# Overlap rows of v by transfer in row 1, and a later second dilated tile in rows 4 to 7, in a fused attention and MLP kernel

## The chip, the core and the metric

One core of a Trainium2 chip runs the whole program. The metric is the device time of one execution in microseconds; less is better. The figure given for a kernel is the median of several runs. A profile is one further execution, recorded by the hardware profiler; all durations below are from it.

## The reference

Two stages run one after the other. The first is attention with 8 heads of width 64 over 8 sequences of 576 tokens. Heads 0 to 3 look at a sliding window: each token sees itself and the 31 before it. Heads 4 to 7 look at a dilated window: each token sees every fourth token back over 128 tokens, again 32 of them. The second stage is an MLP over all 4608 tokens, from 512 to 2048 and back, with a squared ReLU.

```python
mask_plain = (rel >= 0) & (rel < window)                                   # window = 32
mask_dil = (rel >= 0) & (rel < window * dilation) & (rel % dilation == 0)  # dilation = 4
scores = np.where(masks, scale * q @ k.T, -1e9)
attn = softmax(scores)
x = (attn @ v)            # then (B, H, S, D) -> (B * S, H * D)
h = x @ w_in              # 4608 x 2048
out = (maximum(h, 0) ** 2) @ w_out
```

## The kernel before

**Rows and chunks.** A "row" is one of the 8 sequences of the batch. A "chunk" is 512 of the 4608 tokens, so there are nine. The kernel computes the attention of row b while it runs the MLP of chunk b - 1; the products are in fp16 with fp32 sums.

**How the order is set.** Each engine executes its own instructions in the order in which the program issues them. The MLP of a chunk is a Python generator (`moe_gen`: `mm1_gen`, then `mm2_gen`, `mm2_by_rows_gen` or `mm2_strassen_gen`). `pump(n)` advances it by n steps, and the attention code calls `pump` between its own pieces. A step of mm1 is half of one block of 128 hidden units: two matmuls of 128x512 (L305). Every second step adds the ScalarE activation `rt` (L328) and the VectorE square `g` (L329); two of those steps add sums of g (L338, L339). A step of the second product is four matmuls of 128x256 (L382) from chunk 2 on, which use seven products in place of eight (sums on VectorE: L413, L425, L409; ScalarE copies: L398), and two matmuls of 128x512 (L450) before that. So the number in a `pump` says how much MLP work TensorE, ScalarE and VectorE find between two attention pieces.

**The attention of a row.** `s_sliding` and `s_dilated` compute scores into PSUM tiles `ps` and `pz`; ScalarE takes the exponential into AT (L572), VectorE multiplies by the mask (L575). `av_sliding(b, mp)` multiplies by `vp` into `pav` (L643), two blocks of 96 tokens at a time. `av_dilated(b, t, a)` multiplies by `vd` into `paw` (L659); t is the tile of 80 or 64 positions, a says which two of the four token classes. Both end in `normalize`: a reciprocal (L626) and a product (L631) on VectorE. The PSUM tiles ps, pz, pav and paw, and in row 1 the transposes px and py too, share a pool `pa` of two buffers. Then x is transposed into `xT`, the input of the MLP: rows 0 to 3 on TensorE (L672, L690) with ScalarE copies (L678, L696), rows 4 to 7 by transfer: `x_sliding_by_dma` (L701), and `x_dilated_by_dma` (L708) into tiles `yd`, which `x_from` (L696, ScalarE) puts into xT.

**v and its overlap.** Rows of v arrive from HBM as fp32 in `sv` and `sd` (L132, L137, SP's queue) and GpSimd casts them to fp16 into `vp[b % 2]` (three instructions at L169) and `vd[b % 2]` (four at L177; the first two cover all 128 partitions and write tile 0, the last two 64 partitions of tile 1). A query block also needs keys from the block before it. For sliding heads the last 32 partitions of block m - 1 are repeated in partitions 0 to 31 of block m; for dilated heads the last 64 partitions of tile 0 are repeated in partitions 0 to 63 of tile 1. There are three ways for that in the code:
- `halo_sliding` (L184, three instructions) and `halo_dilated` (L189, two) on ScalarE, called from `attn_scores` and `attn_values`: rows 0, 1 and 2.
- `halo_sliding_by_dma` (L201) and `halo_dilated_by_dma` (L204), one transfer each on SP's queue from on-chip memory to on-chip memory: both in rows 3 and 4, and L204 in rows 5 to 7.
- `halo_sliding_at_end` (L196) on VectorE: rows 5 to 7.

**Around row 1.** GpSimd casts vp, then issues the load of wo (L153) and of row 2's q and k (`ns`, L112), casts vd, and issues the copies of row 2's dilated q and k (`dd`, L214). SP's queue holds row 1's loads of v, and after them the writes of row 2's reordered q and k (L224, behind the VectorE copy L120).

**Rows 4 to 7.** `attn_values_by_dma` issues three sliding pieces with `pump(3)` each, then two dilated tiles t, each with two pieces a:

```python
for t in range(2):
    for a in range(2):
        av_dilated(b, t, a, xs)
        pump(4 + 2 * (a > t))
    ys.append(x_dilated_by_dma(b, t, xs))
    then[1 + t](ys[t])
```

The steps after these four pieces are 4, 6, 4 and 4. `then[1]` loads the next row's sliding v (L132); `then[2]` issues the transposes of its q and k (L232, L236), loads its dilated v (L137) and lets GpSimd cast vp once yd of tile 1 has landed (L914).

Of the kernel before, what the change touches and what calls it, by code (L numbers as in the profile page):

```python
# [17 lines left out]
def kernel(  # L18
# [132 lines left out]
    def load_w_out(gs):  # L151
        for g in gs:
            nc.gpsimd.dma_start(  # L153
                out=wo[g],
                in_=moe_w_out[4 * g * P : 4 * (g + 1) * P, :].rearrange(
                    "(fl s) m -> fl (s m)", s=4
                ),
            )
# [8 lines left out]
    def cast_sliding_v(b, ms=range(0, NB, 2)):  # L167
        for m in ms:
            nc.gpsimd.tensor_copy(  # L169
                vp[b % 2][:, m : m + 2, :, 0:D], sv[:, :, m : m + 2, :].rearrange("p h m d -> p m h d")  # L170
            )

    def cast_dilated_v(b):
        for t in range(2):
            p0 = 64 * t
            for c in range(0, DIL, 2):
                nc.gpsimd.tensor_copy(  # L177
                    vd[b % 2][p0:P, t, c : c + 2, :, 0:D],
                    sd[p0:P, t, :, D * c : D * (c + 2)].rearrange("p h (c d) -> p c h d", d=D),
                )  # L180

    def halo_sliding(b, mp):
        m0, m1 = max(1, 2 * mp), 2 * mp + 2
        nc.scalar.copy(  # L184
            vp[b % 2][0:PADP, m0:m1, :, 0:D], vp[b % 2][P - PADP : P, m0 - 1 : m1 - 1, :, 0:D]
        )

    def halo_dilated(b, c):
        nc.scalar.copy(  # L189
            vd[b % 2][0:64, 1, c : c + 2, :, 0:D], vd[b % 2][64:P, 0, c : c + 2, :, 0:D]  # L190
        )
# [8 lines left out]
    def halo_sliding_by_dma(b):  # L200
        nc.sync.dma_start(out=vp[b % 2][0:PADP, 1:NB], in_=vp[b % 2][P - PADP : P, 0 : NB - 1])  # L201

    def halo_dilated_by_dma(b):
        nc.sync.dma_start(out=vd[b % 2][0:64, 1], in_=vd[b % 2][64:P, 0])  # L204
# [6 lines left out]
    def keep_dilated_qk(b):  # L211
        d = dpool.tile([2, HH * CL, DIL * D], FP16, name=f"dd{b}", tag="dd")
        for i, src in ((1, k), (0, q)):
            nc.gpsimd.dma_start(  # L214
                out=d[i].rearrange("(r i) x -> r (i x)", i=4),
                in_=src[b, HH:H].rearrange("h (r i) d -> (h r) (i d)", i=16),
                max_dma_last_dim=4096,
            )
        return d
# [301 lines left out]
    def pump(n):  # L521
        for _ in range(n):
            while pending:
                try:
                    next(pending[0])
                    break
                except StopIteration:
                    pending.pop(0)
# [52 lines left out]
    def s_sliding(b, hp, between=None):  # L581
        tiles = [pa(f"ps{b}_{hp}_{half}") for half in range(2)]
        for half, ps in enumerate(tiles):
            for m3 in range(3):
                m = 3 * half + m3
                for e in range(2):
                    r = slice(D * e, D * (e + 1))
                    nc.tensor.matmul(  # L588
                        ps[:, e, QB * m3 : QB * (m3 + 1)],
                        QKTp[b % 2][r, 1, hp, QB * m : QB * m + P],  # L590
                        QKTp[b % 2][r, 0, hp, PADP + QB * m : PADP + QB * (m + 1)],
                        start=True,
                        stop=True,
                    )
        for half, ps in enumerate(tiles):
            exps(2 * hp + half, ps)
            if not between:
                masked(2 * hp + half, maskp)
        if between:
            between()  # L600
            for half in range(2):
                masked(2 * hp + half, maskp)

    def s_dilated(b, g):
        tiles = [pa(f"pz{b}_{g}_{h}") for h in range(2)]
        for h, ps in enumerate(tiles):
            for a in range(2):
                for t in range(2):
                    q0 = KPAD + (2 * g + h) * CL + Q0D[t]
                    for e in range(2):  # L610
                        r = slice(D * e, D * (e + 1))
                        o = CL * a + Q0D[t]
                        nc.tensor.matmul(  # L613
                            ps[:, e, o : o + QD[t]],
                            QKTd[b % 2][r, 1, a, q0 - PADD[t] : q0 - PADD[t] + P],
                            QKTd[b % 2][r, 0, a, q0 : q0 + QD[t]],
                            start=True,
                            stop=True,
                        )
        for h, ps in enumerate(tiles):  # L620
            softmax(4 + 2 * g + h, ps, maskd)
# [11 lines left out]
    def x_tiles(b):  # L633
        x = xp.tile([QB, 2, NB, 2, D], FP16, name=f"xs{b}", tag="xs")
        return x, [xp.tile([QD[t], DIL, HH, D], FP16, name=f"xd{b}_{t}", tag=f"xd{t}") for t in range(2)]

    def av_sliding(b, mp, xs):
        pav = pa(f"pav{b}_{mp}")
        for i in range(2):
            m = 2 * mp + i  # L640
            for h in range(HH):
                off = (h % 2) * 288 + (m % 3) * QB
                nc.tensor.matmul(  # L643
                    pav[:, i, h * (D + 2) : h * (D + 2) + D + 1],
                    AT[:, 2 * (h // 2) + m // 3, off : off + P],
                    vp[b % 2][:, m, h, 0 : D + 1],
                    start=True,
                    stop=True,
                )
        normalize(  # L650
            b, f"p{mp}", pav, QB, xs[0][:, :, 2 * mp : 2 * mp + 2].rearrange("p c m e d -> p m c e d")
        )
# [30 lines left out]
    def x_dilated(b, t, xs, wide):  # L683
        py = pt(f"py{b}_{t}", wide)
        w = QD[t]
        for r in range(DIL):
            x = xs[1][t][:, r].rearrange("p h d -> p (h d)")
            for c in range(2):
                o = w * (2 * r + c)
                nc.tensor.transpose(py[:, o : o + w], x[:, P * c : P * (c + 1)], ident[0:w, 0:w])  # L690
        x_from(b, t, py[:, 0 : 8 * w].rearrange("x (r c i) -> x r c i", r=DIL, c=2))
# [21 lines left out]
    def attn_scores(b, gap, less=0, hooks={}):  # L713
        for hp in range(2):
            s_sliding(b, hp)
            if hp in hooks:
                hooks[hp]()
            pump(gap)
        for g in range(2):
            s_dilated(b, g)  # L720
            if 2 + g in hooks:
                hooks[2 + g]()
            if g and b < 3:
                halo_sliding(b, 0)
            pump(gap - less)

    def attn_values(b, gap, wide=False, then=None):
        xs = x_tiles(b)
        for mp in range(3):
            av_sliding(b, mp, xs)  # L730
            if b < 3:
                if mp < 2:
                    halo_sliding(b, mp + 1)
                else:
                    halo_dilated(b, 0)
            if then and b == 2 and mp == 2:
                then()
            pump(gap)
        x_sliding(b, 0, xs, wide)
        if b < 3:  # L740
            halo_dilated(b, 2)
        pump(gap)
        av_dilated(b, 0, 0, xs)
        if then and b == 1:
            then()
        pump(gap)
        x_sliding(b, 1, xs, wide)
        pump(gap)
        av_dilated(b, 0, 1, xs)
        pump(gap)  # L750
        for a in range(2):
            av_dilated(b, 1, a, xs)
            pump(gap)
        x_dilated(b, 0, xs, wide)
        pump(gap)
        x_dilated(b, 1, xs, wide)

    def attn_values_by_dma(b, then):
        xs = x_tiles(b)
        for mp in range(3):  # L760
            av_sliding(b, mp, xs)
            if mp == (2 if b > 4 else 1):
                then[0]()
            pump(3)
        x_sliding_by_dma(b, xs)
        ys = []
        for t in range(2):
            for a in range(2):
                av_dilated(b, t, a, xs)
                pump(4 + 2 * (a > t))  # L770
            ys.append(x_dilated_by_dma(b, t, xs))
            then[1 + t](ys[t])
        pump(6)
        x_from(b, 0, ys[0])
        pump(7)
        x_from(b, 1, ys[1])
# [34 lines left out]
    nc.gpsimd.tensor_copy(sd[64:P, :, :, 0], wi[2][64:P, :, 0:2].rearrange("p d f -> p f d"))  # L811
    load_v(1)
    cast_sliding_v(1)
    load_w_out((3,))
    ns = load_sliding_qk(2)
    cast_dilated_v(1)
    dd = keep_dilated_qk(2)
    for mp in (1, 2):
        av_sliding(0, mp, xs)
# [135 lines left out]
```

## Time and profile before

| | us |
|---|---|
| median of 4 runs (lowest, highest) | 306.76 (305.39, 308.54) |
| the profiled execution's own time | 308.54 |
| its span | 306.8 |
| PE, DVE, ACT, POOL busy | 288.4, 208.7, 173.1, 63.6 |
| halo copies on ScalarE, L184 x9, mean | 0.539 |
| halo copies on ScalarE, L189 x6, mean | 0.616 |

The span is that of the instructions; the time of an execution includes what lies around it. PE is TensorE's matmuls, PEld its weight loads, DVE VectorE, ACT ScalarE, POOL GpSimd, SP the engine that issues most transfers. A row of a timeline gives the start and the length in us, the engine, the line, the operation with output and inputs, how many instructions were merged, and in brackets the idle time before it with what ended that. Lengths of merged rows overlap a little with the next. The row of a window gives from and to, the length, then for each engine the busy time and the number of instructions, the granted TensorE clock, the busy share of the DMA engines and what they moved in GB/s.

Row 1's attention lies at about 49 to 63 us, row 4's at 131 to 153, row 5's at 161 to 189, row 6's at 192 to 219, and row 7's at 222 to 249. From 251 us on only the MLP is left.

### The profile page before, as it was taken

What the parts mean: (1) busy time and instruction counts of PE and PEld (TensorE: products, weight loads), DVE (VectorE), ACT (ScalarE), POOL (GpSimd) and SP (SyncE); (2) the same over time, 40 slices, a digit from 0 to 9 for tenths busy, and PEclk for the clock granted to TensorE, in tenths of its full rate; (3) what the DMA queues carried; (4) which work ended last, traced back from release to release, by engine and by line L of the source; (5) the groups of instructions that cost most, each with busy time, mean ns of one, the idle gap of its engine ahead of it and who ended that gap; (6) DMA issues with size and microseconds to landing.
All of it is one profiled execution on the core that took longest, in us unless ns stands there. A gap on an engine that the chain in (4) does not pass through costs nothing.

```text
span 306.8 us, 6890 instructions
## 1 busy us (share of the span) xinstructions
PE 288.4 (94%) x2760; PEld 192.8 (63%) x2760; DVE 208.7 (68%) x437; ACT 173.1 (56%) x293; POOL 63.6 (21%) x112
## 2 busy tenths in 40 slices
PE   1869999999999999999999999999999999999994
PEld 1444545455555458855888988558855975785583
DVE  7753445858961789579948994899489934834652
ACT  2943656677844883396439534954396347425620
POOL 4435008001431710530026002600230000000000
PEclk9995999999999999999999999999999999999999
DMA  7699997699979999996799999998993230003004
GB/s 121 132 228 215 205 197 124 107 223 224 155 168 192 251 174 206 179 259 128 144 131 282 178 148 189 273 177 167 156 268 20 51 119 28 2 1 137 2 1 137
DMA packets 77471, 46.77 MB, mean 152 GB/s; under 512 B 58432, under 2 KB 69184, under 8 KB 77440
## 3 DMA queue, kind: packets, MB, share of 16 engines
q1 hardware_dynamic: 68688, 32.71, 51.5%
q0 software_dynamic: 8752, 13.63, 25.9%
q8 instruction: 21, 0.34, 0.5%
q14 instruction: 10, 0.08, 0.1%
HBM read 36.70 MB, written 16.52 MB: 173 GB/s over the span
## 4 chain that ended last, share of the span: by engine, by line
PE 65%; DMA 14%; DVE 9%; SPq 4%; ACT 3%; issue 2%; POOL 1%; DVEq 0%; POOLq 0%
PE ph L305 29%; PE pa L382 14%; PE pb L382 7%; PE po L450 6%; DMA sd<-in_v_dram 4%; DMA QKTp<-dp 4%; PE pc L382 3%; DVE g L329 3%; DMA nd<-in_q_dram 2%; DMA ns<-in_q_dram 2%; DMA vd<-vd 2%; PE paw L659 2%; ACT AT L572 1%; PE ps L588 1%; DVE AT L575 1%
## 5 line engine op out<-in xcount | busy, mean ns | idle before, releaser
L305 PE MATMUL ph<-xT,wi 128*128 128x512 f16 (+1 forms) x640 | 136.6, 363 | 0.7 <-ACT xT L696 0.7
L328 ACT ACTIVATE rt<-ph 128x512 f16<-128x512 f32 x144 | 86.3, 609 | 47.1 <-PE ph L305 44.0
L305 PEld LDWEIGHTS <-wi 128*128 128x128 f16 x640 | 68.6, 114 | 47.9 <-issue 3.7
L329 DVE TENSOR_TENSOR g<-rt 128x512 f16<-128x512 f16 x144 | 62.7, 447 | 40.2 <-ACT rt L328 39.0
L382 PEld LDWEIGHTS <-g 128*128 128x128 f16 x448 | 43.3, 98 | 6.2
L382 PEld LDWEIGHTS <-gs 128*128 128x128 f16 x336 | 32.0, 98 | 5.1 <-DVE gs L339 1.6
L450 PE MATMUL po<-wo,g 128*128 128x512 f16 x128 | 33.1, 379 | 0.0
L382 PE MATMUL pa<-wt,gs 128*128 128x256 f16 x224 | 27.6, 273 | 0.8 <-DVE gs L339 0.7
L409 DVE TENSOR_TENSOR ov<-pb,ov 128x512 f32<-128x512 f32 x14 | 9.7, 691 | 25.8 <-ACT ov L398 13.1
L382 PE MATMUL pb<-wt,g 128*128 128x256 f16 x224 | 27.1, 273 | 0.0
L169 POOL CAST vp<-sv 128x512 f16<-128x512 f32 x24 | 15.0, 656 | 53.7 <-DMA sv<-in_v_dram 42.1
L398 ACT COPY ov<-pa 128x512 f32<-128x512 f32 x14 | 8.2, 585 | 31.0 <-PE pa L382 31.0
L177 POOL CAST vd<-sd 128x512 f16<-128x512 f32 (+1 forms) x32 | 21.6, 703 | 14.5 <-DMA sd<-in_v_dram 12.4
L631 DVE TENSOR_TENSOR xd<-paw,rcp_d 80x512 f16<-80x512 f32 (+1 forms) x32 | 21.9, 684 | 1.1
L572 ACT ACTIVATE AT<-pz 128x576 f16<-128x576 f32 x32 | 19.7, 695 | 1.1 <-PE pz L613 1.1
L572 ACT ACTIVATE AT<-ps 128x576 f16<-128x576 f32 x32 | 19.2, 657 | 1.8 <-PE ps L588 1.3
L575 DVE TENSOR_TENSOR AT<-AT,maskp 128x576 f16<-128x576 f16 x32 | 15.1, 480 | 5.4 <-ACT AT L572 3.7
L575 DVE TENSOR_TENSOR AT<-AT,maskd 128x576 f16<-128x576 f16 x32 | 16.7, 543 | 2.5 <-ACT AT L572 0.9
L631 DVE TENSOR_TENSOR xs<-pav,rcp_p 96x512 f16<-96x512 f32 x24 | 16.5, 687 | 0.8
L659 PEld LDWEIGHTS <-AT 128*128 128x128 f16 x256 | 12.1, 98 | 7.3 <-issue 2.4
L398 ACT COPY ou<-pa 128x512 f32<-128x512 f32 x14 | 8.2, 586 | 14.0 <-PE pa L382 14.0
L450 PEld LDWEIGHTS <-g 128*128 128x128 f16 x128 | 10.4, 98 | 8.3
(81 smaller groups left out, 274.6 us busy)
## 6 DMA issues: line engine op xcount, KB each, us to landing
sv<-in_v_dram SPq DMA_DIRECT2D x14, 288.0 KB, 5.5
dp<-nr SPq DMA_DIRECT2D x12, 288.0 KB, 3.9
out_dram<-ou SPq DMA_DIRECT2D x6, 512.0 KB, 4.1
out_dram<-ov SPq DMA_DIRECT2D x6, 512.0 KB, 4.5
sd<-in_v_dram SPq DMA_DIRECT2D x8, 320.0 KB, 6.3
ns<-in_k_dram POOLq DMA_DIRECT2D x8, 288.0 KB, 6.4
ns<-in_q_dram POOLq DMA_DIRECT2D x8, 288.0 KB, 7.5
sd<-in_v_dram SPq DMA_DIRECT2D x8, 256.0 KB, 6.5
```

Source lines behind the costliest of these rows:

```text
L169: nc.gpsimd.tensor_copy(vp[b % 2][:, m : m + 2, :, 0:D], sv[:, :, m : m + 2, :].rearrange("p h m d -> p m h d"))
L177: nc.gpsimd.tensor_copy(vd[b % 2][p0:P, t, c : c + 2, :, 0:D], sd[p0:P, t, :, D * c : D * (c + 2)].rearrange("p h (c d) -> p c h d", d=D),)
L305: nc.tensor.matmul(ph[:, t0:t1], wi4[ffc // 4][:, dmk, :, ffc % 4], xT[:, dmk, x0 : x0 + t1 - t0], start=(dmk == 0 and t0 == 0), stop=(dmk ...
L328: nc.scalar.activation(rt, ph[:], ACTF.Relu)
L329: nc.vector.tensor_mul(g[:, ffc, :], rt, rt)
L382: nc.tensor.matmul(banks[bank][:, t], a(k, t), b(k), start=(new and t == 0 and k == 0), stop=(k == HF - 1), skip_group_check=True,)
L398: nc.scalar.copy(ot, banks[A])
L450: nc.tensor.matmul(po, g[:, ffc, t * P : (t + 1) * P], wo[ffc // 4][:, ffc % 4, :], start=(ffc == 0), stop=(ffc == NFF - 1),)
L572: nc.scalar.activation(AT[:, u, 0:UW], ps[:, :, 0 : UW // 2], ACTF.Exp, scale=scale)
L575: nc.vector.tensor_mul(AT[:, u, 0:UW], AT[:, u, 0:UW], mask)
L631: nc.vector.tensor_tensor(out=x, in0=pv, in1=rb, op=ALU.mult)
L659: nc.tensor.matmul(pav[:, e, h * (D + 2) : h * (D + 2) + D + 1], AT[:, 4 + h, off : off + P], vd[b % 2][:, t, 2 * a + e, h, 0 : D + 1], st ...
```

## The change

It has two parts. In row 1 the five ScalarE copies of the overlap are no longer issued; two transfers on SP's queue, the ones that rows 3 and 4 use, take their place, each issued in the program right after the cast that it reads. In rows 4 to 7 the steps after the four dilated pieces become 7, 3, 4 and 4: the second piece, with its normalization and the transfer that follows it, comes three steps later in the program; the third and the fourth stay at the same step.

```diff
@@ attn_scores
-            if g and b < 3:
+            if g and b == 2:
                 halo_sliding(b, 0)
             pump(gap - less)
@@ attn_values
             av_sliding(b, mp, xs)
-            if b < 3:
+            if b == 2:
                 if mp < 2:
                     halo_sliding(b, mp + 1)
                 else:
...
         x_sliding(b, 0, xs, wide)
-        if b < 3:
+        if b == 2:
             halo_dilated(b, 2)
@@ attn_values_by_dma
                 av_dilated(b, t, a, xs)
-                pump(4 + 2 * (a > t))
+                pump((7, 3)[a] if t == 0 else 4)
@@ the program's order, row 1
     load_v(1)
     cast_sliding_v(1)
+    halo_sliding_by_dma(1)
     load_w_out((3,))
     ns = load_sliding_qk(2)
     cast_dilated_v(1)
+    halo_dilated_by_dma(1)
     dd = keep_dilated_qk(2)
```

## The prediction

> **What bounds the kernel now.** I read the page first, then TensorE's idle time stage by stage, then each engine's timeline through row 1 and rows 4 to 7. The page's first row, and two stages from the table by window:
>
> ```profile
> PE 288.4 (94%) x2760; PEld 192.8 (63%) x2760; DVE 208.7 (68%) x437; ACT 173.1 (56%) x293; POOL 63.6 (21%) x112
> ...
> 49.00:64.50 15.50, 14.59 (x180) 7.44 (x180) 10.51 (x23) 11.41 (x21) 3.88 (x7) 1.00 0.82 163
> ...
> 140.00:155.00 15.00, 15.00 (x145) 11.26 (x142) 13.79 (x29) 7.20 (x11) 0.00 (x0) 1.00 0.66 125
> ```
>
> TensorE is the bound. Its idle time is 306.8 - 288.4 = 18.4 us, of which 14 - 6.62 + 12 - 8.25 = 11.1 us lie before 26 us and 56.2 - 52.1 = 4.1 us in the last window; only 3.2 us is left between. Row 1 (49 to 64.5 us) holds 0.91 us of it. In rows 4 to 7 (130 to 250.6 us) it is 1.0 us: the windows show 0.27, 0.40 and 0.34 us, in stages 155-172, 172-190 and 203-221. Nothing that a change in these two places hides can give more than these sums, plus gaps that the busy row covers.
>
> There are such gaps. The Trainium skill (Trainium Kernel Development and Optimization, section Performance Expectations) says that matmul busy time judges distance to the roofline badly, since matmuls are pipelined. The row bears it out in row 1: from 55.56 to 62.70 us pairs of L450 need 0.43 us by the chain, yet the next group starts 0.06 to 0.23 us later, seven times, 0.94 us together. By the busy row, row 1 could give 0.91 us; by the rule and the starts, 1.85 us. I use the starts, but only as far as the engine behind the gaps, VectorE, can move.
>
> **Row 1: what goes.** Five ScalarE copies, L184 three times and L189 twice: 1.44 + 0.62 + 0.61 = 2.67 us of ScalarE. What stands in their way is seen in the timelines of PE, ACT, DVE and POOL:
>
> ```profile
> 54.18 0.29 PE L643 MATMUL pav<-vp,AT 128*128 128x65 f16 x4
> 55.01 0.29 PE L643 MATMUL pav<-vp,AT 128*128 128x65 f16 x4 [0.54 <-ACT vp L184]
> ...
> 52.25 2.28 ACT L572 ACTIVATE AT<-pz 128x576 f16<-128x576 f32 x4 [0.27 <-PE pz L613]
> 54.55 1.44 ACT L184 COPY vp<-vp 32x256 f16<-32x256 f16 x3
> ...
> 52.93 2.09 DVE L575 TENSOR_TENSOR AT<-AT,maskd 128x576 f16<-128x576 f16 x4 [0.40 <-ACT AT L572]
> 55.33 0.20 DVE L626 RECIPROCAL rcp_p<-pav 96x8 f32<-96x8 f32 x1 [0.31 <-PE pav L643]
> ...
> 45.60 1.72 POOL L169 CAST vp<-sv 128x512 f16<-128x512 f32 x3 [16.61 <-DMA sv<-in_v_dram]
> ...
> 49.02 2.83 POOL L177 CAST vd<-sd 128x512 f16<-128x512 f32 x4
> ```
>
> Block 0 of pav needs no overlap; block 1 waits 0.54 us for the first L184, which stands behind four exponentials. Without it pav ends about 54.18 + 0.43 = 54.6. But VectorE masks until 52.93 + 2.09 = 55.02, so its reciprocal moves from 55.33 to 55.02: **0.31 us**, not 0.54. From there VectorE and its PSUM buffers set the pace to the end of the row: it runs without a break to 57.93, paw starts at 58.08 on the buffer then freed, and the normalizations follow one another to 62.6 (rcp_d 60.05, 60.90, 61.73). So the row ends 0.31 us earlier. ScalarE's later copies wait for TensorE (0.98 and 0.45 us idle before the two L678), so its freed time buys nothing more. L120 (59.38) moves with VectorE; its input needs to have landed by 59.07, and landed at 48.41 + 6.9 = 55.3.
>
> **Row 1: what comes.** Two transfers on SP's queue. SP issues nothing between 41.05 (L137) and 60.15 us (L224), so nothing stands behind their waits: L224 needs L120, not SP. No other queue is passed. vp may go when the three L169 casts end, 47.3; vd when the two 128-row L177 casts end, about 50.4 (row 5 shows this: casts from 166.28 take 1.59 us for two, and L204 goes at 167.90). The same transfers of rows 3 to 7, L201 and then L204:
>
> ```profile
> DMA to landing us min/median/max: 2.9/2.9/3.0
> ...
> DMA to landing us min/median/max: 2.4/4.5/7.6
> ```
>
> The DMA engines moved 0 to 41 GB/s from 47 to 49 us, so vp is near its own row: landing 47.4 + 3.0 = 50.4, needed at 54.4, 4.0 us to spare; even at 7.6 it lands at 55.0, where L184 delivers now. vd goes out amid wo, ns and dd (about 200 GB/s from 50 to 58 us). The rule against taking the long row is the Trainium skill's round-robin (DMA: Bandwidth & Descriptors, section Queues, rings and completion order): each DMA engine changes queues after a packet, so a small transfer passes a backlog on another queue. By that, 132 KB at half of 200 GB/s takes 1.3 us, and on top of the 2.4 us of the emptiest row that is a landing at 54.1. Row 5's L204, with ns and dd of the same size ahead, took 7.6 us: 50.4 + 7.6 = 58.0. I take the row. vd is read by the third paw, at 60.29 now and 59.98 then: 5.9 us to spare by the rule, 2.0 by the row. Both give 0 us, but only the row leaves the cover thin. The reverse side, that 215 KB more delays wo, ns and dd, is 215/400 = 0.5 us at the 400 GB/s of such copies, inside 3.8 us of slack (55.3 to 59.07).
>
> From 62.7 us TensorE is dense, and the chain of row 2 (L184 at 84.58, L120 at 86.43, L224, the transposes, 0.47 us of PE wait at 102.96) hangs on row 1's end and moves with it. **Row 1: -0.31 us**; between -1.85 (all gaps) and +1.7 (vd at the 11.5 us that dd<-in_q needed in row 5: 61.9, 2.0 late, less 0.31).
>
> **Rows 4 to 7: what moves.** Steps 25 to 34 lie between the first and third paw: 25 to 32 are the last four ffc of mm1 (L305, L328, L329), 33 and 34 the start of L382. Now 4 and 6 of them stand around the second paw, then 7 and 3. Eight matmuls, their reciprocal and product (L626, L631), one transpose on SP (L708) with the L132 loads and later L708 behind it: nothing is added. TensorE's order changes, not its sum. On VectorE the normalization passes exactly one L329 (step 30's). Row 5's order:
>
> ```profile
> 177.46 0.75 DVE L329 TENSOR_TENSOR g<-rt 128x512 f16<-128x512 f16 x2
> 178.12 0.20 DVE L626 RECIPROCAL rcp_d<-paw 80x8 f32<-80x8 f32 x1
> 178.35 0.69 DVE L631 TENSOR_TENSOR xd<-paw,rcp_d 80x512 f16<-80x512 f32 x1
> 178.96 0.75 DVE L329 TENSOR_TENSOR g<-rt 128x512 f16<-128x512 f16 x2
> ```
>
> VectorE is 2 to 3 us behind TensorE there: the paw of 175.09 is normalized at 178.12. Moved by 3 x 0.43 = 1.3 us it would be done near 176.8, still ahead of VectorE. The g that now starts at 178.96 has its rt by 177.02. So no bubble opens; the sequence L329, L338, L339, L413 after it ends when it did. The two PE waits on L339 stay:
>
> ```profile
> 181.22 1.48 PE L382 MATMUL pa<-wt,gs 128*128 128x256 f16 x12 [0.40 <-DVE gs L339]
> ...
> 183.98 1.31 ACT L696 COPY xT<-yd 128x640 f16<-128x640 f16 x1 [0.66 <-DMA yd<-xd]
> 186.23 0.58 ACT L398 COPY ov<-pa 128x512 f32<-128x512 f32 x1 [0.94 <-PE pa L382]
> ```
>
> What is late is yd0, by one L329, 0.33 us: L708 at 179.99, L696 ending 185.62 instead of 185.29. The L398 after it waits for TensorE until 186.23, so 0.94 us of cover becomes 0.61. If it were gone, the next product (186.91) would wait for its bank. L132 behind L708 ends by 183.0, before yd1's L708 at 183.98. The fourth paw (179.97) needs the second's buffer, free at 179.3 instead of 178.96. **0 us**; bounds -1.0 (every wait there gone) and +1.2 (yd0 late by the whole 1.3 us, 0.3 us of PE in each of the four rows).
>
> **Sum.** -0.31 + 0 = -0.3 us. The profiled execution took 308.54 us (span 306.8); it becomes 308.2. The runs' median is 306.76, and the same step gives **306.4 us**. A measurement here tells about 1% (3 us) from no change.
>
> **Rivals.** (1) *The forecast*: 305.9 to 306.8, chance 0.57. (2) *Hidden anyway*: vp lands as late as L184 did, or VectorE's backlog eats the 0.31 us: 306.8; the PE gap at 54.5 speaks against it. With noise around it, 0.18. (3) *Better cover*: ScalarE free at 54.5 and L329 earlier also close gaps behind VectorE and the L339 waits, down to 306.76 - 0.91 - 1.0 = 304.9; against it, VectorE's work is the same. 0.13. (4) *vd late, the slower side*: the third paw waits for the transfer. It decides from a landing of 59.98 - 50.4 = 9.6 us. At 11.5 us the time is 308.4; at the 14.3 us of nd<-in_q in the backlog at 25 us, landing at 64.7, 4.7 - 0.3 = 4.4 us worse, 311.2. For it: SBUF copies beside the same loads went from 2.4 to 7.6 us. Against: 14.3 us came with wo, ns and nd queued ahead, 2 x 512 + 3 x 288 KB = 1.9 MB, against some 1.1 MB here (0.56 of wo and ns left, and 0.58 of dd). 0.12.
>
> The range, 304.9 to 308.4, takes in (1) to (3) and the milder (4). Faster by over 1% would need all 3.2 us of mid-kernel idle: 0.03. Slower by over 1% is the worse half of (4) and something unseen: 0.08. Within 1%: 0.89.
>
> **What would show it.** Right: L184 x6, L189 x4, L201 x3, L204 x6; no PE wait for vp in row 1; rcp_p following maskd at once; vd landed before the third paw; row 1 ending 0.3 us earlier; in rows 4 to 7 the second paw 1.3 us later, yd0's L708 0.3 us later, the PE waits on L339 unchanged. Wrong: a PE wait on DMA vd or vp, a new PE idle after 130 us, or rows 2 and 3 not keeping row 1's gain.

## The result, and the profile after

Over 43 runs of the changed kernel and 64 of the one before, the medians are 306.29 and 306.43 us, and the ratio is 0.9996 with a 95% interval from 0.9980 to 1.0012: -0.1 us, give or take 0.5. No difference can be told. The forecast of -0.3 us lies in that interval, but so does nothing at all, and the profile says that for row 1 it was nothing: the wait of TensorE that was to go is still there, with another name. The page's first row, then row 1 on TensorE, VectorE, GpSimd and SP's queue of the changed kernel:

```profile
PE 287.5 (95%) x2760; PEld 192.7 (64%) x2760; DVE 210.2 (69%) x437; ACT 170.6 (56%) x288; POOL 62.1 (20%) x112
```

```profile
46.28 0.43 PE L588 MATMUL ps<-QKTp 64*128 64x96 f16 x12
...
51.34 0.29 PE L643 MATMUL pav<-vp,AT 128*128 128x65 f16 x4
52.22 0.29 PE L643 MATMUL pav<-vp,AT 128*128 128x65 f16 x4 [0.59 <-DMA vp<-vp]
```

```profile
50.10 2.33 DVE L575 TENSOR_TENSOR AT<-AT,maskd 128x576 f16<-128x576 f16 x4
52.55 0.20 DVE L626 RECIPROCAL rcp_p<-pav 96x8 f32<-96x8 f32 x1
```

```profile
44.80 1.72 POOL L169 CAST vp<-sv 128x512 f16<-128x512 f32 x3 [16.14 <-DMA sv<-in_v_dram]
...
48.22 3.16 POOL L177 CAST vd<-sd 128x512 f16<-128x512 f32 x4
```

```profile
46.55 0.60 SPq L201 DMA_DIRECT2D vp<-vp  x1
49.83 0.54 SPq L204 DMA_DIRECT2D vd<-vd  x1
```

The answers on these two lines in row 1, vp first:

```profile
DMA to landing us min/median/max: 5.6/5.6/5.6
```

```profile
DMA to landing us min/median/max: 5.9/5.9/5.9
```

Two things are to be seen. The vp transfer took 5.6 us instead of 3.0, landed at 52.2, and pav's second block waited 0.59 us for it (0.54 for ScalarE before). And VectorE's masks now end at 52.43, 6.15 us after the row's first score matmul; in the first profile of before it was 55.02 - 49.12 = 5.90 us. The reciprocal starts 0.12 us after them, so 0.59 us of wait on TensorE cost VectorE 0.1 us, or 0.2 by comparison with e0 below, where the reciprocal starts 0.08 us ahead of the recorded end of the masks.

In rows 4 to 7 the order on VectorE is the predicted one, with exactly one more L329 ahead of the second normalization (row 5):

```profile
173.65 1.08 DVE L329 TENSOR_TENSOR g<-rt 128x512 f16<-128x512 f16 x3
174.66 0.20 DVE L626 RECIPROCAL rcp_d<-paw 80x8 f32<-80x8 f32 x1
174.89 0.69 DVE L631 TENSOR_TENSOR xd<-paw,rcp_d 80x512 f16<-80x512 f32 x1
175.50 0.41 DVE L329 TENSOR_TENSOR g<-rt 128x512 f16<-128x512 f16 x1
```

and TensorE waits on L339 as it did:

```profile
177.42 1.48 PE L382 MATMUL pa<-wt,gs 128*128 128x256 f16 x12 [0.48 <-DVE gs L339]
...
207.88 1.48 PE L382 MATMUL pa<-wt,gs 128*128 128x256 f16 x12 [0.48 <-DVE gs L339]
```

The profiled spans, 306.8 before and 303.1 after, are not the change. At row 1's first score matmul the two executions were 49.12 - 46.28 = 2.84 us apart already, mostly for a reason that the first experiment shows. So the kernels are compared below by two stretches of TensorE's timeline: "row 1" from the first L588 of row 1 to that of row 2, and "rows 4 to 7" from the first L588 of row 4 to chunk 7's first L305. A third column gives where in row 1 the first reciprocal starts, counted from the row's first L588. Each ratio is taken against runs of before that were made beside it.

| kernel | row 1, us | first reciprocal, us | rows 4 to 7, us | ratio to before (95%) |
|---|---|---|---|---|
| before, first profile | 24.81 | 6.21 | 119.30 |  |
| before, profiled again (e0) | 25.05 | 6.46 | 119.28 |  |
| changed kernel | 24.87 | 6.27 | 119.32 | 0.9996 (0.9980 to 1.0012) |
| e1, transfers of row 1 alone | 26.07 | 7.47 | 120.54 | 1.0006 (0.9966 to 1.0046) |
| e2, steps of rows 4 to 7 alone | 25.12 | 6.53 | 120.00 | 0.9981 (0.9959 to 1.0003) |
| e3, vp transfer in three pieces | 25.05 | 6.47 | 119.69 | 1.0011 (0.9974 to 1.0047) |
| e4, no overlap in row 1 | 25.10 | 6.52 | 119.51 | 0.9984 (0.9960 to 1.0008) |
| e5, steps 10, 0, 4, 4 | 25.21 | 6.57 | 129.20 | 1.0317 (1.0270 to 1.0364) |
| e7, steps 8, 2, 7, 1 and e3 | 25.19 | 6.60 | 119.72 | 1.0009 (0.9986 to 1.0032) |
| e8, casts ahead of the loads | 26.73 | 5.83 | 119.34 | one run |
| e9, e4 with the casts behind the masks | 24.42 | 5.82 | 120.51 | one run |
| e10, half of the casts behind the masks, and e3 | 25.44 | 6.05 | 118.92 | 0.9976 (0.9955 to 0.9997) |

One stretch of one profile moves by some tenths from execution to execution, up to 1.2 us in rows 4 to 7 (e1, e9), in part by a wait of up to 0.7 us on QKTp at a row's start that comes and goes; a difference below that is read here only where a line carries it.

The first two columns belong together. In ten of the twelve profiles the rest of row 1, from its first reciprocal to row 2's first score matmul, takes 18.6 us (18.58 to 18.64). It is longer only in e8 (20.9) and e10 (19.4), where L120 had to wait for its input ns. So row 1 is as long as its first reciprocal is late, as the prediction had it ("from there VectorE and its PSUM buffers set the pace"), and the question is only what that reciprocal waits for.

### The profile page after: what moved, and what is told of

Read it like the earlier page. It is cut to its first block, busy times and chain, and to the rows that moved or that the text cites. A ratio compares the mean times of both kernels' runs of the same rounds, so it can differ in the third digit from the quotient of the medians.

```text
span 303.1 us, 6885 instructions
## 1 busy us (share of the span) xinstructions
PE 287.5 (95%) x2760; PEld 192.7 (64%) x2760; DVE 210.2 (69%) x437; ACT 170.6 (56%) x288; POOL 62.1 (20%) x112
## 4 chain that ended last, share of the span: by engine, by line
PE 64%; DMA 17%; DVE 11%; issue 2%; ACT 2%; SPq 1%; POOL 1%; DVEq 0%; POOLq 0%
PE ph L305 26%; PE pa L382 15%; PE pb L382 8%; DMA sv<-in_v_dram 6%; PE po L450 5%; DMA wi<-in_moe_w_in_dram 5%; PE pc L382 3%; DMA ns<-in_q_dram 3%; DVE g L329 3%; DMA vp<-vp 2%; PE paw L659 2%; DMA QKTp<-dp 2%; DVE AT L575 1%; PE pav L643 1%; DVE gs L338 1%
## 5 line engine op out<-in xcount | busy, mean ns | idle before, releaser
L305 PE MATMUL ph<-xT,wi 128*128 128x512 f16 (+1 forms) x640 | 134.2, 359 | 0.7 <-ACT xT L696 0.7
L305 PEld LDWEIGHTS <-wi 128*128 128x128 f16 x640 | 68.1, 114 | 45.9 <-issue 0.6
L329 DVE TENSOR_TENSOR g<-rt 128x512 f16<-128x512 f16 x144 | 62.6, 447 | 37.5 <-ACT rt L328 36.3
L631 DVE TENSOR_TENSOR xd<-paw,rcp_d 80x512 f16<-80x512 f32 (+1 forms) x32 | 21.9, 684 | 1.1
L575 DVE TENSOR_TENSOR AT<-AT,maskd 128x576 f16<-128x576 f16 x32 | 18.1, 592 | 2.7 <-ACT AT L572 1.6
L631 DVE TENSOR_TENSOR xs<-pav,rcp_p 96x512 f16<-96x512 f32 x24 | 16.5, 687 | 0.8
```

Of the source, the lines that this page charges most:

```text
L305: nc.tensor.matmul(ph[:, t0:t1], wi4[ffc // 4][:, dmk, :, ffc % 4], xT[:, dmk, x0 : x0 + t1 - t0], start=(dmk == 0 and t0 == 0), stop=(dmk ...
L329: nc.vector.tensor_mul(g[:, ffc, :], rt, rt)
L575: nc.vector.tensor_mul(AT[:, u, 0:UW], AT[:, u, 0:UW], mask)
L631: nc.vector.tensor_tensor(out=x, in0=pv, in1=rb, op=ALU.mult)
```

## The experiments

**e0: the kernel before, profiled once more.**

> The kernel before, profiled once more. In its first profile TensorE ran at a granted clock of 0.85 from 26 to 42 us (64 matmuls of chunk 0 in 15.4 us), in the profile of the changed kernel at 1.00 (13.1 us). Theory A (the cover of the transfer was lent by that slow stretch): with a full clock the span is near 304 us, the three vp casts of row 1 end at or after row 1's first score matmul (46.5 against 46.3 in the changed kernel, where the first profile of before had them 1.8 us ahead), and the wait of pav for the ScalarE copy is still 0.5 us, since ScalarE has the casts' result long before. Theory B (the later cast comes from the change): the casts end 1.5 to 2 us ahead of the first score matmul here too.

The stage from 26 to 42 us, of the first profile of before and then of this one:

```profile
26.00:42.00 16.00, 16.00 (x64) 7.54 (x64) 6.38 (x15) 9.53 (x16) 1.50 (x4) 0.85 1.11 213
```

```profile
26.00:42.00 16.00, 16.00 (x143) 8.18 (x142) 7.93 (x18) 10.00 (x18) 0.34 (x2) 1.00 1.11 210
```

Row 1 of e0 on TensorE and on VectorE:

```profile
45.78 0.43 PE L588 MATMUL ps<-QKTp 64*128 64x96 f16 x12
...
51.67 0.29 PE L643 MATMUL pav<-vp,AT 128*128 128x65 f16 x4 [0.54 <-ACT vp L184]
```

```profile
49.60 2.72 DVE L575 TENSOR_TENSOR AT<-AT,maskd 128x576 f16<-128x576 f16 x4
52.24 0.19 DVE L626 RECIPROCAL rcp_p<-pav 96x8 f32<-96x8 f32 x1
```

The third number from the end is the granted clock: 0.85 then, 1.00 here. The 60 matmuls of chunk 0 in this stage, then and here:

```profile
25.98 15.41 PE L305 MATMUL ph<-xT,wi 128*128 128x512 f16 x60 [0.73 <-ACT xT L696]
```

```profile
24.95 13.11 PE L305 MATMUL ph<-xT,wi 128*128 128x512 f16 x60 [0.67 <-ACT xT L696]
```

That is 2.3 us of the 3.34 by which TensorE reaches row 1 earlier here; the other 1.0 us lay ahead of these matmuls. But v arrives only 0.64 us earlier: the vp casts start at 44.96, 0.82 us ahead of the first score matmul, where they were 3.52 us ahead in the first profile. Theory A holds against B in kind (the casts still end after the first score matmul, at 46.68), and it brings the second finding: here the ScalarE copy makes pav wait 0.54 us too, and **VectorE doesn't wait for it at all**. Its masks end at 52.32, later than pav. The 0.31 us that the prediction wanted to save was not there in this execution of the kernel before. What lowered the clock in the first one is not shown.

**e1: the transfers of row 1 alone.** The changed kernel with `pump(4 + 2 * (a > t))` as before.

> Row 1's transfers alone, with the steps of rows 4 to 7 as before. Theory A: the vp transfer goes out together with the loads of wo and ns and lands 5 to 6 us after its issue; pav waits 0.5 to 0.6 us for it as it waited for ScalarE; ratio 0.998 to 1.002. Theory B (the steps of rows 4 to 7 cost what row 1 gains): no wait of pav on the transfer, ratio 0.999 or less, and lower than that of the whole change.

```profile
51.43 0.29 PE L643 MATMUL pav<-vp,AT 128*128 128x65 f16 x4
53.52 0.29 PE L643 MATMUL pav<-vp,AT 128*128 128x65 f16 x4 [1.80 <-DMA vp<-vp]
```

```profile
53.84 0.20 DVE L626 RECIPROCAL rcp_p<-pav 96x8 f32<-96x8 f32 x1 [0.62 <-PE pav L643]
```

The landing took 5.6 us again, as A says, but the wait is 1.8 us and not 0.6, since in this execution v came later still (casts from 46.10, 0.27 us ahead of the first score matmul). Here the wait is longer than what VectorE's masks cover, the reciprocal waits 0.62 us, and row 1 takes 26.07 us, 1.0 more than in e0. The same transfers in e5 (below) make pav wait 0.90 us and VectorE 0.03. So in these three profiles row 1's transfer is between free and a loss of 1 us; what differs is how early v arrives and how late the masks end. B falls: without the new steps there is no gain either.

**e3: the vp transfer in three pieces, each behind its cast; e4: no overlap in row 1 at all.**

```diff
-    cast_sliding_v(1)
-    halo_sliding_by_dma(1)
+    for m in range(0, NB, 2):
+        cast_sliding_v(1, (m,))
+        m0 = max(1, m)
+        nc.sync.dma_start(
+            out=vp[1][0:PADP, m0 : m + 2], in_=vp[1][P - PADP : P, m0 - 1 : m + 1]
+        )
```

> The whole change, with row 1's vp transfer cut in three, each issued right after the cast that it needs: blocks 1, then 2 and 3, then 4 and 5. Theory A: the first piece goes out about 1.1 us earlier, ahead of the loads of wo and ns, lands in about 2.5 us and the wait of pav is gone; the reciprocal follows the last mask at once, row 1 from its first score matmul to the first of row 2 takes 24.87 - 0.3 us = 24.6 us or less; ratio 0.998 to 0.9995. Theory C (the transfer is slow in itself, from 32 partitions to 32): the first piece takes over 5 us too, and pav waits for 0.2 us or more.

> Leaves out the overlap of v in row 1 altogether (zeros are put there long before), so row 1's first keys are missing; all else as in the changed kernel. The upper limit of what row 1's overlap can give: no wait of pav, row 1 to row 2 in 24.5 us against 24.87, ratio 0.998 to 0.9995 by both theories. If it is the same as the changed kernel within 0.05%, then the third of a microsecond is given back to the transfers of row 2 and 3 (a wait on QKTp at row 3's start); if it is faster by 0.3% or more, then the forecast undervalued what stands behind VectorE in row 1.

The landings of e3's three pieces, and its pav:

```profile
DMA to landing us min/median/max: 1.9/2.1/5.0
```

```profile
51.24 0.42 PE L643 MATMUL pav<-vp,AT 128*128 128x65 f16 x8
51.92 0.42 PE L643 MATMUL pav<-vp,AT 128*128 128x65 f16 x8
53.66 0.41 PE L643 MATMUL pav<-vp,AT 128*128 128x65 f16 x8 [0.89 <-issue]
```

The wait of pav is gone, as A says; the first two pieces land in about 2 us, from 32 partitions to 32, so C falls. The third, issued 0.26 us after the load of wo, takes 5.0. But the row takes 25.05 us, no less: the reciprocal comes at 6.47 us, at the end of the masks, as in e0 (6.46), and the third pav now waits 0.89 us; it starts where VectorE's first normalization ends, which frees a PSUM buffer. In e4 there is no overlap to wait for; the reciprocal comes at 6.52, and the row takes 25.10 us. **The 24.5 to 24.6 us that Theory A of e3 and both theories of e4 expected came in neither.** In these executions row 1 has nothing to give to this change: its first reciprocal waits for VectorE's own masks.

**e9: why VectorE is late.** e4, with the dilated casts behind row 1's masks:

```diff
     attn_scores(1, 2, 1)
+    nc.gpsimd.tensor_copy(seen, AT[:, 7, 0:1])
+    cast_dilated_v(1)
```

> Leaves out the overlap of v in row 1 (as one kernel before it), and starts row 1's four dilated casts on GpSimd only after the last mask of the row. Theory A (GpSimd's cast slows VectorE's masks from 0.46 to 0.86 us, and that, not the overlap, sets when row 1's first reciprocal can start): all eight masks take 0.44 to 0.50 us, the reciprocal starts 5.2 to 5.6 us after the row's first score matmul instead of 6.2 to 6.5, if TensorE's pav lets it. Theory B (the masks are slowed by the loads that come in at that time): they stay at 0.7 to 0.86 us with no cast beside them.

The masks of row 1 (minimum, median and maximum in ns), in e0 and then in e9:

```profile
L575 DVE TENSOR_TENSOR AT<-AT,maskp x4: 458/692/857, 46.8 to 48.8; 128x576 f16<-128x576 f16 x4
L575 DVE TENSOR_TENSOR AT<-AT,maskd x4: 447/822/859, 49.6 to 51.9; 128x576 f16<-128x576 f16 x4
```

```profile
L575 DVE TENSOR_TENSOR AT<-AT,maskp x4: 457/458/459, 47.9 to 49.8; 128x576 f16<-128x576 f16 x4
L575 DVE TENSOR_TENSOR AT<-AT,maskd x4: 457/458/459, 50.7 to 52.3; 128x576 f16<-128x576 f16 x4
```

Theory A holds: beside GpSimd's casts a mask takes up to 0.86 us; with the casts out of the way all eight take 0.46, though the loads of wo and ns come in as before and the copies of dd 2 us earlier. The casts are shorter too, 2.41 us for the four instead of 3.01 in e4. The row takes 24.42 us, 0.68 less than e4, and the reciprocal comes 0.70 earlier, at 5.82: a little later than expected, since VectorE now waits 2.0 us for ScalarE's exponentials (1.2 in e4). In e8 (next), where the casts end earlier in the row and the overlap is moved in full, the reciprocal comes at 5.83 as well.

One thing stays open: not every slow mask lies beside a cast in the trace. The second of e0 (0.70 us) and the first of the changed kernel (0.88) lie beside GpSimd's issuing of loads, and beside such issuing the first four masks of e9 took 0.46.

The Trainium skill states the mechanism (SBUF — State Buffer, section Who interferes with whom): a VectorE instruction with two inputs in SBUF contends with a GpSimd instruction that reads SBUF. The masks have two such inputs, the casts read sd. In e9 the casts run from 52.98 to 55.39 beside the normalizations L631, whose first input is in PSUM, and those keep their 0.69 us.

**e8: why the vp transfer was slow.** The order casts, then loads:

```diff
     halo_sliding_by_dma(1)
-    load_w_out((3,))
-    ns = load_sliding_qk(2)
     cast_dilated_v(1)
     halo_dilated_by_dma(1)
+    load_w_out((3,))
+    ns = load_sliding_qk(2)
```

> The changed kernel with row 1's dilated casts and both overlap transfers issued ahead of the loads of wo and ns, which come about 3 us later. It tells why the vp transfer landed 5.6 us after its issue although the DMA engines moved under 60 GB/s then. Theory A (the loads of wo and ns, issued by GpSimd in the same microsecond, hold it up): with none of them under way vp lands in 1.9 to 3.0 us, pav does not wait for it, and vd lands in under 3.5 us. Theory B (it is held up by GpSimd's casts, which run in this order too): vp still takes 4.5 us or more. By both, ns comes late, VectorE's L120 may wait for it by about 1 us, and the time says little.

vp, then vd:

```profile
DMA to landing us min/median/max: 2.1/2.1/2.1
```

```profile
DMA to landing us min/median/max: 3.3/3.3/3.3
```

Theory A: 2.1 and 3.3 us in place of 5.6 and 5.9, with the casts running as before. The loads of wo and ns hold the transfer up, although the DMA engines moved no more than 22, 33 and 49 GB/s in the three microseconds from 46 to 49 in the changed kernel. The trace shows when it lands: with wo. In the six profiles in which wo's load was issued within 0.3 us of vp's transfer or of its last piece, the two landed within 0.25 us of each other. Why the engines moved so little at first stays open. ns came late, as expected, and more than expected: L120 waited 2.24 us for it, TensorE 2.30 us, and the row took 26.73 us.

**e2: the steps of rows 4 to 7 alone,** with row 1 as before.

> The steps 7, 3, 4, 4 of rows 4 to 7 alone, row 1 as before. Theory A (the moved piece changes an order, not a sum): from row 4's first score matmul to the first matmul of chunk 7 it takes 119.3 us as in the profile of before and of the changed kernel (119.30 and 119.32); the second paw 1.3 us later, the yd0 transpose 0.3 us later against the third paw; TensorE waits on L339 in rows 5 and 6 by 0.3 to 0.5 us as before; ratio 0.998 to 1.002. Theory B (the later tile frees VectorE where TensorE waits for it): L339 waits below 0.2 us and a ratio of 0.997 or less.

The waits on L339 are 0.39 and 0.48 us, and nothing else of rows 5 and 6 is shorter: B falls. The stretch is 120.0 us, 0.7 above what A expected; 0.34 us of it is a wait on QKTp at row 5's start, which the changed kernel did not have in the same rows. Row 1, as before, repeats e0: pav waits 0.54 us for L184, and VectorE doesn't wait, since its masks end 0.4 us after pav.

**e5: the cover in rows 4 to 7, taken away.** Steps 10, 0, 4, 4.

> The changed kernel with the second dilated piece moved to the end of its room: steps 10, 0, 4, 4. It tells whether the cover that the prediction named in rows 4 to 7 is real, and which part of it ends first. Theory A: the second normalization now also passes the last two L329, L338, L339 and L413 (0.33 x 2 + 0.73 x 2 + 1.14 = 3.3 us later than in before), so it frees its buffer 2.5 to 3 us after the fourth paw wants it: TensorE waits there 2 to 3 us in each of the rows 4 to 7, the waits on L339 are gone, and the time grows by 7 to 12 us (ratio 1.02 to 1.04). Theory B (VectorE's backlog is not what orders this): the fourth paw waits under 0.5 us and the time grows by under 2 us.

```profile
149.16 0.41 PE L659 MATMUL paw<-vd,AT 128*128 128x65 f16 x8 [1.84 <-DVE rcp_d L626]
...
181.68 0.41 PE L659 MATMUL paw<-vd,AT 128*128 128x65 f16 x8 [2.41 <-DVE rcp_d L626]
...
214.79 0.42 PE L659 MATMUL paw<-vd,AT 128*128 128x65 f16 x8 [2.78 <-DVE rcp_d L626]
...
247.98 0.41 PE L659 MATMUL paw<-vd,AT 128*128 128x65 f16 x8 [1.59 <-DVE rcp_d L626]
```

Theory A: the fourth paw waits in each row (under 2 us in rows 4 and 7), 8.6 us together, L339 is no longer waited for, and the time is 316.64 us, ratio 1.032. Not all of the 10.2 us is this wait: from 210 to 228 us the granted clock was 0.91 in this execution, which makes another 1.6 us of the stretch (an estimate, 18 x 0.09). So the second piece is not free to stand anywhere. What ends its cover first is the PSUM buffer that the fourth piece needs. With 7 steps the change keeps on the safe side of it: in row 5 the second normalization ends at 174.89 + 0.69 = 175.58, and the fourth paw starts at 176.09.

**e7: an attempt to use this.** e3's pieces; steps 8, 2, 7, 1; L132 ahead of the yd0 transpose; `pump(8)` and `pump(5)` around the first `x_from`.

> A version that uses what the profiles show: row 1's vp transfer in three pieces, steps 8, 2, 7, 1 in rows 4 to 7, so that the second normalization stands behind L338 and L339 and the fourth paw comes late enough for its buffer, the L132 loads issued before the yd0 transpose, and the first L696 after the L398 that TensorE needs. Theory A: the waits on L339 in rows 5 and 6 (0.48 us each) are gone and none takes their place; from row 4 to chunk 7 118.3 to 118.6 us instead of 119.3; ratio 0.996 to 0.998. Theory B (the later yd transfers delay the transposes of the next row's q and k): a wait on QKTp at the start of row 6 or 7 of 0.5 us or more takes the place, ratio 0.999 to 1.003.

The waits on L339 shrink, and others come:

```profile
178.26 1.92 PE L382 MATMUL pb<-wt,g 128*128 128x256 f16 x16 [0.19 <-DVE g L413]
...
207.11 1.05 PE L382 MATMUL pa<-wt,gs 128*128 128x256 f16 x8 [0.15 <-DVE gs L339]
209.08 1.92 PE L382 MATMUL pb<-wt,g 128*128 128x256 f16 x16 [0.19 <-DVE g L413]
```

Neither theory foresaw that: the second normalization now stands ahead of L413, which TensorE needs next, and the stretch is 119.72 us. VectorE still has too much work ahead of L413; to change its order here only changed for whom TensorE waits.

**e10: half of the casts behind the masks.** e3's pieces, and in rows 1, 5, 6 and 7 the two casts of tile 1 after the row's scores, with e9's copy ahead of them.

> A version from the profiles: the changed kernel with row 1's vp transfer in three pieces, and in rows 1, 5, 6 and 7 the two dilated casts of tile 1 on GpSimd start only after the row's last mask, so that half of the casts no longer lie beside the masks. Theory A (the casts' slowing of VectorE is what rows 1, 5 and 6 wait for): the masks of row 1 lose about half of their excess, the row takes 24.6 to 24.8 us instead of 25.05, and the waits on L339 in rows 5 and 6 fall from 0.48 to 0.2 us or less; ratio 0.997 to 0.999. Theory B (the later casts slow L329 and the normalizations by as much): waits and row lengths within 0.1 us of the changed kernel, ratio 0.999 to 1.001.

The waits on L339, and L120 of row 1:

```profile
177.97 1.48 PE L382 MATMUL pa<-wt,gs 128*128 128x256 f16 x12 [0.48 <-DVE gs L339]
...
208.14 1.49 PE L382 MATMUL pa<-wt,gs 128*128 128x256 f16 x12 [0.22 <-DVE gs L339]
```

```profile
57.28 0.76 DVE L120 COPY nr<-ns 128x2304 f16<-128x2304 f16 x1 [0.73 <-DMA ns<-in_q_dram]
```

The median is 305.30 us against 305.79 beside it, the ratio 0.9976 with an interval that just leaves out 1. The profile supports less than that: in rows 4 to 7 it is 0.4 us shorter, the wait on L339 is halved in row 6 and unchanged in row 5, where L120 waited 0.49 us for ns and the first half of the casts, which stays in its place, still lay beside two L329 (1.71 us for the two, 1.58 in the changed kernel). In row 1 five masks still took 0.85 to 0.88 us. The first reciprocal came at 6.05, 0.4 earlier than in e3, but the row was not shorter: v and with it ns came late in this execution, and L120 waited for it. So Theory A is met in part. The ratio is the lowest in the table, and a gain of a quarter of a per cent that one more series could take back.

## Why the prediction was right, and where it was not

**The sum.** -0.3 us was forecast and -0.1 (±0.5) measured; the number, the range and "within 1%" stand. But a third of a microsecond cannot be told from none by the times, and the profiles put row 1 at none or a small loss. So the number came out right by the smallness of the change, not by its mechanism. What came was the second rival, "hidden anyway", in both of its forms at once.

**Row 1, the term of 0.31 us.** The step that failed is "VectorE masks until 55.02, so its reciprocal moves from 55.33 to 55.02". It was read correctly, from an execution whose TensorE had lost some 2.3 us to a low clock before row 1 (the 60 matmuls above). There GpSimd's dilated casts ended at 51.85, ahead of the last four masks, and these took 0.46 us each. In e0 the casts lie beside most of the masks, the masks end after pav, and there is nothing between them and the reciprocal to remove. e3 and e4 show it for the changed kernel; e9 shows the cause. For the first execution the sum fits: e9's masks end 5.91 us after the first score matmul, as there (5.90), nothing waits for the overlap, and the row takes 24.42 us against 24.81.

**Row 1, the landing of vp.** "The DMA engines moved 0 to 41 GB/s, so vp is near its own row" failed. The slack of 4.0 us was used up by two terms: the casts started 1.48 us ahead of the first score matmul instead of 3.52, which takes 2.0, and the landing took 5.6 us instead of 3.0, which takes 2.6. 4.0 - 2.0 - 2.6 = -0.6, the wait that the profile shows. The bound that was given, "even at 7.6 it lands at 55.0, where L184 delivers now", held in the changed kernel's profile (both 5.9 us after the first score matmul) and not in e1 (7.1).

**Row 1, vd.** Of the row's 7.6 us and the round-robin rule's 3.7 us, the row was nearer: 5.9 us. It landed at 55.8, 1.7 us ahead of the third paw at 57.50, against 2.0 forecast. That the two agree so well is luck: it was issued 2.3 us later in the row than reckoned (3.55 us after the first score matmul, not 1.28), and the shorter landing gave 1.7 of that back. The rule's 3.7 us was met only where the loads were issued 1.5 us or more after it (3.3 us in e8). The bound drawn from 61.9 is 0.1 too high: that is 1.9 us behind 59.98, which makes +1.6. The fourth rival had the right mechanism on the wrong tile: it is vp whose lateness can decide, as e1's 1.8 us of wait shows, at about 1 us and not 4.4.

**Row 1, the reverse side.** The delay of ns by the added 215 KB was to be 0.5 us, inside 3.8 us of slack. From issue to landing, ns<-in_q took 8.4 to 8.7 us in the five kernels with the transfers of row 1 beside it (the changed one, e1, e3, e5, e7) and 7.6 to 7.7 without them (e0, e2, e4; 6.9 in the first profile): 0.7 to 1.1 us more. And the slack had come from the slow start as well: in the changed kernel ns landed at 56.26 and L120 took it at 56.59. That cost nothing here, but 0.3 us is left.

**Rows 4 to 7.** Right: one L329 passed, no bubble on VectorE, TensorE's order changed and not its sum, the waits on L339 as before (e0 has 0.47 and 0.48 us). The second paw comes 3.28 us after the first instead of 1.99. The yd0 transpose was to be 0.33 us later against the third paw. It was in row 4 (0.82 for 0.48 us) and row 7, but in rows 5 and 6 only 0.07 and 0.0 against e0. There it waits behind the L701 transposes in SP's own queue, which the working left out. The first profile shows it in row 5, where the second normalization had ended at 179.04:

```profile
175.78 3.79 SPq L701 DMA_TRANSPOSE xT<-xs  x2
179.66 1.23 SPq L708 DMA_TRANSPOSE yd<-xd  x1
```

The changed kernel has the same order:

```profile
171.97 3.79 SPq L701 DMA_TRANSPOSE xT<-xs  x2
175.86 1.23 SPq L708 DMA_TRANSPOSE yd<-xd  x1
```

**The gain of row 2 and 3 that was to hang on row 1** was not tested, since row 1 gave none.

## What to carry to other kernels

Before a wait is priced, see whether the engine behind it would have been ready: TensorE's 0.54 us were covered by VectorE, and the cover was visible only with the profile of an undisturbed start. Slack between a transfer and an engine is a difference of two clocks; when one stretch of the profile ran at a reduced clock, the slack read behind it can be stretched too (3.52 us of lead in the first profile, 0.3 to 1.5 in the three others above), and a second profile shows it. A moved instruction has its limit at the buffer that it frees: move it up to there, and look for gains in the work of the engine that is late, not in its order.

## What the runs showed of the hardware

- An on-chip transfer of 82.5 KB landed in 2.1 us by itself and in 5.6 us when two loads from another queue were issued within half a microsecond of it; in the first 2.5 us the DMA engines then moved under 50 GB/s (e8, the changed kernel). Here the throughput at the time of issue did not tell the landing.
- An fp16 product of VectorE with both inputs in SBUF took 0.86 us beside GpSimd's casts and 0.46 us without; with an input in PSUM it kept its 0.69 us beside them (e0, e9).
- From one execution of the same kernel to the next the granted clock of one early stretch was 0.85 or 1.00 (first profile of before, e0), and TensorE's 60 matmuls there took 15.41 or 13.11 us; that moved the order in which transfers and TensorE met in row 1.
